# Three waiting score tiles move out of the shared wide slots, and the planner's DMA factor goes from 1.1 to 0.9

## The chip, the cores and the metric

One core of one Trainium2 chip runs the whole program. The metric is the device time of one execution in microseconds (us), taken as the median of several executions without a profiler. One further execution, recorded by the hardware profiler, gives the trace that is read here.

## The reference

Eight sequences of 3072 tokens go through an attention unit without a softmax and then through a maxout layer. Cut to what matters:

```python
# u, v: [8, 3072, 256]   z: [8, 3072, 64]   w1, w2: [256, 1024]   w_out: [1024, 256]
scores = (1 / 3072) * z @ z.T                 # per sequence, symmetric
attn   = maximum(scores, 0) ** 2
x      = u * (attn @ v)                       # [8 * 3072, 256]
out    = maximum(x @ w1, x @ w2) @ w_out      # [24576, 256]
```

## The kernel before

**Steps.** A sequence is cut into six groups of 512 tokens (four blocks of 128). One step computes one group's rows of the output, so there are 48 steps, n = 0 to 47, and sequence b = n // 6, group s = n % 6. The score matrix is symmetric: a block of scores that step i computes for a later group j (i < j) is transposed by a DMA (a "turn", job `("turn", n, k0)`, an SP instruction) and read again in step j. Only a few blocks of sequence 0 are computed directly instead (`direct`).

**A step's work.** TensorE (PE) makes score pairs `s_ps` (two blocks of 128 x 512, one PSUM pair), ScalarE (ACT) or VectorE (DVE) applies the relu into an A tile (`a_sb`, line 276 or 278) and one of them squares it in place (lines 282, 284). SP turns the squares into a T tile (`aT`), two turns for a tile of four blocks. Steps 0 to 2 are "plain": PE multiplies v by the A tiles directly. From step 3 on, the products follow a Strassen-like scheme with seven products for eight: DVE makes sums `es` of the A and T tiles (jobs S2, S3, S4, lines 290 and 293; S3 writes back into the tile), and PE runs products `Xa`, `Xb`, `Ya`, `Yb` over the step's six groups into `acc`. `add_ends` makes xT = u * acc; `add_second` or `add_seven` does the maxout layer for the step LAG = 3 behind: relu tiles `g_sb`, in most steps sums of them in `gs`, and the output tile `o_sb`, which SP stores to `out`. For b = 0 the turned tiles are those of (0,3), (0,4), (0,5), (1,3), (1,4), (1,5), (2,3), (2,4), (2,5), (3,4), (3,5), (4,5), where (i,j) is computed in step i and read in step j. Tiles of step 3 and later are turned after their S3, those of the plain steps right after the square.

**Buffers.** A tiles and T tiles of 4 KB per partition share WIDE = 19 slots (`share_wide`): by the planner's modelled times each tile gets the slot that comes free first, and it waits for all users of the tile that had the slot before. The output pool `opool` has two buffers of the same size, used in rotation (first by a staging tile `zf`, then by the output tiles of steps 0, 1, 2, ...). The pool `gspool` has one buffer for `gs`.

**Held tiles.** With HELD = 1, the tiles (0,4) and (0,5) of step 0 are called held: they take wide slots of their own (`a_held`), and the T tiles for them are ordered as if taken one microsecond into step 2 (`at_step(0, key[1] + 2, 1)`). Their turns may so be issued late, while the A tile keeps its slot.

**Planner.** PE's order is written out by hand (`pe_order`). All other engines' orders come from a list scheduler in the kernel's Python (`find_orders`): each job has a cost, a lag and a due time worked back from PE's plan, and at each point the job that can start first, or among nearly equal ones the one due first, is put next on its engine. The engines then run their queues in that order, each instruction waiting for its own semaphores. All DMAs, from SP and from POOL (GpSimd, which issues the loads of u, v, z and the weights), share one modelled queue:

```python
dma_free[0] = max(dma_free[0], begin + DMA_START[...]) + DMA_PART * j.dma
j.done = dma_free[0] + DMA_END
idle_from["SP"] = max(begin + SP_ISSUE, dma_free[0] - DMA_AHEAD)   # SP's DMAs only
```

with `DMA["turn"] = 1180` ns, `DMA_START` 870 (SP) or 1770 (POOL), `DMA_END` 1330, `DMA_AHEAD` 4500, `SP_ISSUE` 1450. The plan is made in 24 rounds, and the one that ends first by the model is kept.

Of the kernel before, what the change touches and what calls it, by code (L numbers as in the profile page):

```python
# [11 lines left out]
def kernel(  # L12
# [19 lines left out]
    bf16 = mybir.dt.bfloat16  # L32
# [7 lines left out]
    P = 128  # L40
    NSB = S // P
    G = 4
    WIN = 3
    GW = G * P
# [25 lines left out]
    widepool = ctx.enter_context(tc.tile_pool(name="widepool", bufs=1))  # L70
# [3 lines left out]
    gspool = ctx.enter_context(tc.tile_pool(name="gspool", bufs=1))  # L74
    opool = ctx.enter_context(tc.tile_pool(name="opool", bufs=2))
# [85 lines left out]
    def direct(b, i, j):  # L161
        return b == 0 and i < j <= NDIR
# [16 lines left out]
    q.zT = zpool.tile([P, NSB + 1, P], bf16, name="zT")  # L179


    HELD = 1
    ALONE, XB_TO, YA_FROM, YA_FIRST, O_CLEAR = 4, 2, 2, 6, 2


# [12 lines left out]
    TURN, TURN_LAG, UT_LAG = 1750, 4000, 7000  # L198

    DMA = dict(turn=1180, uT=1130, zT=4220, w2T=3800, store=1940, v=1680, u=1680, z=3130, w1=4100, w2=3000, wo=3500)  # L200
    DMA_SMALL, DMA_PART = 970, 1.1
    DMA_START, DMA_END, DMA_AHEAD, SP_ISSUE = {"SP": 870, "POOL": 1770}, 1330, 4500, 1450
    FIRST_LOADS = {("v", 0, 0): 0, ("v", 0, 1): 1200, ("v", 0, 2): 2500, ("v", 0, 3): 3700, ("v", 0, 4): 4900, ("v", 0, 5): 7700, ("u", 0): 6300}

# [17 lines left out]
    jobs, bufs, order = {}, {}, {}  # L222

    def job(key, ways, fn, deps=(), new=None, uses=(), after=(), lag=100):
        assert key not in jobs, key
        jobs[key] = Job(key, ways, fn, deps, new, uses, after, lag)

    def buf(pool, key, make):
        bufs[pool, key] = Buf(make)
        order.setdefault(pool, []).append(key)  # L230

    def tile_of(pool, key):
        return bufs[pool, key].tile
# [27 lines left out]
    def score(q, out_ps, j, k, s, q0, n):  # L261
        half = ds(j * dqk, dqk)
        matmul(
            out_ps,
            q.zT[half, k + 1 - j, :],
            q.zT[half, ds(G * s + 1 - j + q0, n), :],
            start=True,
            stop=True,
        )

    def turn(out_ap, in_ap):
        sp_dma(out=out_ap, in_=in_ap, transpose=True)

    def relu(eng, out_ap, in_ap):
        if eng == "ACT":
            pin(nc.scalar.activation(out_ap, in_ap, AF.Relu))  # L276
        else:
            pin(nc.vector.tensor_single_scalar(out=out_ap, in_=in_ap, scalar=0.0, op=ALU.max))

    def square(eng, ap):  # L280
        if eng == "ACT":
            pin(nc.scalar.activation(ap, ap, AF.Square))  # L282
        else:
            pin(nc.vector.tensor_mul(ap, ap, ap))  # L284
# [16 lines left out]


    def a_key(n, g):
        return ("T", ("held", n, g)) if n < HELD and g > 3 else ("A", (n, g))

    def a_tile(st, g):
        return tile_of(*a_key(st.n, g))
# [3 lines left out]
    def a_half(tile, k0):  # L311
        return tile[:, ds(k0 % G, 2), :].rearrange("p k x -> p (k x)")

    def a_rows(st, k0):
        return a_half(a_tile(st, k0 // G), k0).rearrange("p (t m x) -> p m t x", t=2, m=2)
# [84 lines left out]
    def s_tile(key):  # L400
        return tile_of("mm", key)

    def by_tokens(s_ps):
        return s_ps.rearrange("p m (t x) -> p m t x", t=2)
# [4 lines left out]
    def add_pair(st, k0, head=None):  # L409
        n, q, g = st.n, st.q, k0 // G  # L410
        key = (n, k0)
        first = k0 % G == 0
        if first:
            if a_key(n, g)[0] == "A":
                buf("A", (n, g), lambda tag: widepool.tile([P, G, GW], bf16, name="a_sb", tag=tag))
            else:
                bufs[a_key(n, g)] = Buf(lambda tag: widepool.tile([P, G, GW], bf16, name="a_held", tag=tag))

        def scores(_):
            for j in range(2):  # L420
                score(q, s_tile(key)[:, j, :], j, k0 + j, st.s, 0, G)

        job(("score", n, k0), {"PE": 223}, scores, deps=z_deps(st), new=("mm", key), lag=150)

        def do_relu(eng):
            relu(eng, a_rows(st, k0), by_tokens(s_tile(key)))

        def do_square(eng):
            square(eng, a_half(a_tile(st, g), k0))

        a = a_key(n, g)
        job(
            ("relu", n, k0),
            RELU,
            do_relu,
            deps=[("score", n, k0)],
            new=a if first else None,
            uses=[("mm", key), a],
            after=() if first else [("relu", n, k0 - 2)],
            lag=200,  # L440
        )
        job(("square", n, k0), SQUARE, do_square, deps=[("relu", n, k0)], uses=[a], lag=200)
        if g > st.s and not direct(st.b, st.s, g):
            t = ("T", (st.b, st.s, g))
            if first:
                turned_order.append((("score", n, k0), t[1]))
                bufs[t] = Buf(lambda tag: widepool.tile([P, G, GW], bf16, name="aT", tag=tag))

            def do_turn(_):
                turned = a_half(tile_of(*t), k0)  # L450
                turn(turned.rearrange("p (s x) -> p s x", x=P), a_half(a_tile(st, g), k0))

            job(
                ("turn", n, k0),
                {"SP": TURN},
                do_turn,
                deps=[("square", n, k0) if first or st.plain else ("S3", n, g)],
                new=t if first else None,
                uses=[a, t],
                after=() if first else [("turn", n, k0 - 2)],  # L460
                lag=TURN_LAG + (5000 if st.plain else 0),
            )
# [467 lines left out]
    def add_seven(st):  # L930
# [111 lines left out]
        for name, ways, fn, deps, after, new, uses in (  # L1042
            ("osn", {"ACT": 470}, lambda e: held(), [("o", n, 1)], [], ok, [pair, ok]),
            ("oe1", {"DVE": 336}, lambda e: sub(C(0, 1), slot(1), C(0, 0)), [("osn", n)], [], None, [pair, ok]),
            ("onf", {"DVE": 336}, lambda e: sub(C(1, 1), C(1, 1), slot(3)), [("o", n, 3)], [], None, [pair, ok]),
            ("ok", {"DVE": 336}, lambda e: add(C(0, 0), C(1, 1), slot(0)), [("onf", n)], [], None, [pair, ok]),
            ("oe3", {"DVE": 336}, lambda e: sub(C(1, 1), slot(1), C(1, 1)), [("onf", n)], [("ok", n)], None, [pair, ok]),
            ("oe0", {"DVE": 336}, lambda e: add(C(0, 0), C(0, 0), slot(2)), [("ok", n)], [("oe3", n)], None, [pair, ok]),
            ("oe2", {"ACT": 270}, lambda e: copy("ACT", C(1, 0), slot(2)), [("o", n, 3)], [], None, [pair, ok]),
        ):  # L1050
            job((name, n), ways, fn, deps=deps, new=new, uses=uses, after=after, lag=200)
# [241 lines left out]
    turned_order = []  # L1293
# [135 lines left out]
    for i, w in enumerate(work):  # L1429
        key = w[2]  # L1430
# [43 lines left out]
    def pe_job_at(ns):  # L1474
        found = [key for key, at in zip(pe_order, pe_at) if at >= ns]
        return [found[0]] if found else [pe_order[-1]]


    def at_step(b, s, us):
        return pe_job_at(starts[NG * b + s] + us * 1000)  # L1480
# [13 lines left out]
    def z_deps(st):  # L1494
        return [("zT", st.b)] if st.b else []
# [130 lines left out]
    for st in steps:  # L1626
        for k0 in st.rows:
            add_diag(st) if k0 is None else add_pair(st, k0)
# [22 lines left out]
    for k0 in (0, 2, 4, 6):  # L1651
        bufs["mm", (0, k0)] = Buf(psum_pair)
    order["mm"] = [(0, k0) for k0 in (0, 2, 4, 6)] + order["mm"]
    for pool in ("acc0", "acc1"):
        order[pool].sort(key=lambda k: k[0] * 2 + k[1] if isinstance(k, tuple) else 2 * k)
    position = {key: i for i, key in enumerate(pe_order)}
    order["A"].sort(
        key=lambda k: position.get(("score", k[0], None if k[1] == steps[k[0]].s and steps[k[0]].diag else G * k[1]), -1)
    )
    def held(key):  # L1660
        return a_key(key[1], key[2] // G)[0] == "T"

    slots = sorted(
        [
            (position[at_step(0, key[1] + 2, 1)[0]] if held(key) else position.get(key, -1), k)
            for key, k in turned_order
        ]
        + [(position.get(key, -1), ("held", key[1], k[2])) for key, k in turned_order if held(key)]
        + [(position[at_step(0, 0, 7)[0]], "w2"), (position[at_step(0, 1, 7)[0]], "w2T")],
        key=lambda x: x[0],  # L1670
    )
# [3 lines left out]
        A=NA, T=NT, es=6, v=6, lf=5, xT=LAG, g=2, o=2, e0=1, gs=1, xs=1, u=2, uT=2, mm=1000, acc0=1, acc1=1  # L1675
# [306 lines left out]
```

## Time and profile before

| | |
|---|---|
| median of 3 executions | 910.29 us (909.14 to 910.53) |
| profiled execution, own time | 914.21 us |
| its span in the trace | 912.4 us |
| mean granted TensorE clock | 0.996 |
| PE / DVE / ACT / POOL busy | 892.1 / 790.0 / 756.2 / 58.4 us |
| DMA moved | 146.65 MB, mean 161 GB/s |

The profiled execution is 3.92 us longer than the median of the executions without a profiler. PE is busy for 98% of the span. A "window" of the profile is a stretch of the span with the busy time of every engine in it; the granted clock there is the share of full TensorE speed. A DMA issue on SP is shown with the time it kept SP's queue, which includes its wait for semaphores; "to landing" is the time from its issue until the data has arrived.

### The profile page before, as it was taken

Reading aid. Unit: us, or ns where it says so; the run is one execution under the profiler, and the core shown is the slowest. Engines: PE = TensorE matmul, PEld = TensorE weight load, DVE = VectorE, ACT = ScalarE, POOL = GpSimd, SP = SyncE. Lnnn points to the kernel's source line nnn. Section 1 sums busy time; section 2 is a strip of 40 time slices with the busy share of each in tenths; the row PEclk is TensorE's granted clock in tenths of the full one; section 3 lists DMA queues with packets and bytes.
Section 4 is the critical chain, followed back from the end, with each engine's and each line's share of the span. In section 5 each row is a group of like instructions: output and inputs, shape, how many; then the busy total and the mean of one; then the engine's idle time right before and its main releaser. Section 6 shows DMA issues by size and latency. Waiting matters only on the chain.

```text
span 912.4 us, 37105 instructions
## 1 busy us (share of the span) xinstructions
PE 892.1 (98%) x16333; PEld 745.5 (82%) x16333; DVE 790.0 (87%) x1703; ACT 756.2 (83%) x944; POOL 58.4 (6%) x115
## 2 busy tenths in 40 slices
PE   9999799999999999999999999999999999999998
PEld 3368688887888888888788888888888898888885
DVE  6777678988989999999899899998999899989970
ACT  7967699778997899888997889977999779997634
POOL 2101000010000000001000010000000001000000
PEclk9999899999999999999999999999999999999999
DMA  9999999999999999999999999999989999999711
GB/s 156 130 167 175 186 182 173 175 163 159 153 169 190 164 183 149 164 185 167 165 146 164 183 169 151 166 169 173 183 138 178 179 178 152 170 160 162 123 61 70
DMA packets 382930, 146.65 MB, mean 161 GB/s; under 512 B 361264, under 2 KB 362928, under 8 KB 382768
## 3 DMA queue, kind: packets, MB, share of 16 engines
q1 hardware_dynamic: 366208, 114.54, 79.3%
q0 software_dynamic: 16560, 29.74, 23.5%
q8 instruction: 127, 2.08, 1.0%
q14 instruction: 35, 0.29, 0.1%
HBM read 59.77 MB, written 25.17 MB: 93 GB/s over the span
## 4 chain that ended last, share of the span: by engine, by line
PE 74%; DVE 12%; DMA 6%; ACT 4%; issue 2%; SPq 0%; POOL 0%; DVEq 0%; POOLq 0%; ACTq 0%
PE s_ps L87 37%; PE acc L87 37%; DMA v_sb<-in_v_dram 3%; DMA aT<-a_sb 3%; DVE es L290 2%; ACT a_sb L276 2%; DVE es L293 2%; DVE a_sb L293 1%; ACT g_sb L276 1%; DVE xT L297 1%; DVE e L290 1%; DVE e L293 1%; DVE a_sb L284 1%; DVE o_sb L293 1%; DVE gs L293 1%
## 5 line engine op out<-in xcount | busy, mean ns | idle before, releaser
L87 PEld LDWEIGHTS <-v_sb 64*128 64x128 bf16 (+1 forms) x4464 | 336.1, 94 | 68.9 <-issue 15.2
L276 ACT ACTIVATE a_sb<-s_ps 128x1024 bf16<-128x1024 f32 x337 | 303.8, 943 | 45.4 <-PE s_ps L87 43.8
L87 PEld LDWEIGHTS <-lf 64*128 64x128 bf16 x3240 | 266.2, 94 | 21.9 <-issue 7.3
L87 PE MATMUL acc<-es,v_sb 64*128 64x256 bf16 x2160 | 279.0, 269 | 0.0
L87 PE MATMUL acc<-es,lf 64*128 64x256 bf16 x1080 | 246.6, 269 | 0.3
L87 PE MATMUL acc<-a_sb,lf 64*128 64x256 bf16 x1224 | 233.1, 269 | 1.0 <-issue 1.0
L87 PE MATMUL s_ps<-xT,w_sb 64*128 64x512 bf16 (+1 forms) x1484 | 214.0, 377 | 0.0
L282 ACT ACTIVATE a_sb<-a_sb 128x1024 bf16<-128x1024 bf16 (+1 forms) x217 | 211.1, 993 | 2.3
L276 ACT ACTIVATE g_sb<-s_ps 128x1024 bf16<-128x1024 f32 x187 | 185.9, 1024 | 8.6 <-PE s_ps L87 6.9
L87 PE MATMUL acc<-aT,lf 64*128 64x256 bf16 x936 | 180.1, 271 | 3.8 <-DMA aT<-a_sb 3.1
L87 PE MATMUL acc<-a_sb,v_sb 64*128 64x256 bf16 (+1 forms) x1352 | 145.4, 280 | 3.2 <-DVE e L290 2.3
L87 PE MATMUL s_ps<-zT 64*128 64x512 bf16 (+2 forms) x774 | 122.5, 337 | 6.1 <-DVE o_sb L290 2.9
L290 DVE TENSOR_TENSOR es<-aT 128x1536 bf16<-128x1536 bf16 (+1 forms) x117 | 106.5, 933 | 1.3 <-DMA aT<-a_sb 1.2
L87 PEld LDWEIGHTS <-gs 64*128 64x128 bf16 x2688 | 99.1, 94 | 9.5 <-issue 1.3
L87 PEld LDWEIGHTS <-w_sb 64*128 64x128 bf16 (+1 forms) x1488 | 80.9, 94 | 26.0 <-POOLq L95 1.0
L87 PEld LDWEIGHTS <-g_sb 64*128 64x128 bf16 x2336 | 91.6, 94 | 10.4 <-POOLq L95 7.1
L284 DVE TENSOR_TENSOR a_sb<-a_sb 128x1024 bf16<-128x1024 bf16 (+1 forms) x121 | 74.8, 625 | 25.9 <-ACT a_sb L276 25.9
L87 PE MATMUL acc<-aT,v_sb 64*128 64x256 bf16 x936 | 89.5, 272 | 0.0
L293 DVE TENSOR_TENSOR es<-a_sb 128x512 bf16<-128x512 bf16 x198 | 79.1, 421 | 9.6 <-PE acc L87 9.5
L87 PE MATMUL s_ps<-wf_sb,gs 64*128 64x128 bf16 x2016 | 81.2, 216 | 0.5 <-issue 0.5
L87 PE MATMUL s_ps<-w_out_sb,g_sb 64*128 64x128 bf16 (+1 forms) x1664 | 78.8, 226 | 0.0
L290 DVE TENSOR_TENSOR es<-a_sb 128x1024 bf16<-128x1024 bf16 x108 | 72.4, 687 | 0.0
(84 smaller groups left out, 1079.6 us busy)
## 6 DMA issues: line engine op xcount, KB each, us to landing
out_dram<-o_sb SPq DMA_DIRECT2D x47, 512.0 KB, 5.5
v_sb<-in_v_dram POOLq DMA_DIRECT2D x48, 256.0 KB, 6.0
u_sb<-in_u_dram POOLq DMA_DIRECT2D x48, 256.0 KB, 5.7
aT<-a_sb SPq DMA_TRANSPOSE x230, 5.3
z_sb<-in_z_dram POOLq DMA_DIRECT2D x7, 384.0 KB, 7.0
w_sb<-in_moe_w_dram POOLq DMA_DIRECT2D x2, 512.0 KB, 10.3
uT<-u_sb SPq DMA_TRANSPOSE x48, 5.6
a_sb<-a_sb SPq DMA_TRANSPOSE x45, 5.5
```

The lines of the kernel that those rows point to most:

```text
L87: newest[0] = pin(nc.tensor.matmul(*args, **kw)).ins
L276: pin(nc.scalar.activation(out_ap, in_ap, AF.Relu))
L282: pin(nc.scalar.activation(ap, ap, AF.Square))
L284: pin(nc.vector.tensor_mul(ap, ap, ap))
L290: pin(nc.vector.tensor_add(*args))
L293: pin(nc.vector.tensor_sub(*args))
L297: nc.vector.scalar_tensor_tensor(out=out_ap, in0=in0, scalar=c2, in1=in1, op0=ALU.mult, op1=ALU.mult)
```

## The change

The tiles (0,4) and (0,5) are now built in `opool`, under the name and in the buffers of the output tiles, and the tile (1,5) of step 1 is built in `gspool`, in the buffer of `gs`. None of the three takes a wide slot any more; (1,5) had an ordinary A slot before. The output tiles of steps 0 and 1 come after (0,4) and (0,5) in the rotation of the output pool, and the first `gs` comes after (1,5). The T tiles for (0,4) and (0,5) are ordered one microsecond into step 1, and the T tile for (1,5) nine microseconds into step 1 (TURNED_AT); before, the one for (1,5) was ordered at the tile's own scores. The planner's factor DMA_PART, by which each transfer's own part of the modelled DMA queue is multiplied, goes from 1.1 to 0.9, for all 48 steps.

```diff
-    HELD = 1
+    HOMES, TURNED_AT = {(0, 4): "o", (0, 5): "o", (1, 5): "gs"}, {0: (1, 1), 1: (1, 9)}
...
-    DMA_SMALL, DMA_PART = 970, 1.1
+    DMA_SMALL, DMA_PART = 970, 0.9
...
     def a_key(n, g):
-        return ("T", ("held", n, g)) if n < HELD and g > 3 else ("A", (n, g))
+        return (HOMES[n, g], ("held", n, g)) if (n, g) in HOMES else ("A", (n, g))
...
-        if first:
-            if a_key(n, g)[0] == "A":
-                buf("A", (n, g), lambda tag: widepool.tile([P, G, GW], bf16, name="a_sb", tag=tag))
-            else:
-                bufs[a_key(n, g)] = Buf(lambda tag: widepool.tile([P, G, GW], bf16, name="a_held", tag=tag))
+        a = a_key(n, g)
+        if first and a[0] == "A":
+            buf("A", (n, g), lambda tag: widepool.tile([P, G, GW], bf16, name="a_sb", tag=tag))
+        elif first:
+            home, name = {"o": (opool, "o_sb"), "gs": (gspool, "gs")}[a[0]]
+            buf(*a, lambda: home.tile([P, G, GW], bf16, name=name))
...
+    for pool in ("o", "gs"):
+        order[pool].sort(key=lambda k: (not isinstance(k, tuple), k))
...
     slots = sorted(
         [
-            (position[at_step(0, key[1] + 2, 1)[0]] if held(key) else position.get(key, -1), k)
+            (position[at_step(0, *TURNED_AT[key[1]])[0]] if a_key(key[1], key[2] // G)[0] != "A" else position.get(key, -1), k)
             for key, k in turned_order
         ]
-        + [(position.get(key, -1), ("held", key[1], k[2])) for key, k in turned_order if held(key)]
```

More of the change, by code (lines that the diff above doesn't have):

```diff
@@ L429, in do_square @@
             square(eng, a_half(a_tile(st, g), k0))
-        a = a_key(n, g)
         job(
@@ L1659 @@
     )
-    def held(key):
-        return a_key(key[1], key[2] // G)[0] == "T"
     slots = sorted(
         [
-            (position[at_step(0, key[1] + 2, 1)[0]] if held(key) else position.get(key, -1), k)
+            (position[at_step(0, *TURNED_AT[key[1]])[0]] if a_key(key[1], key[2] // G)[0] != "A" else position.get(key, -1), k)
             for key, k in turned_order
         ]
-        + [(position.get(key, -1), ("held", key[1], k[2])) for key, k in turned_order if held(key)]
         + [(position[at_step(0, 0, 7)[0]], "w2"), (position[at_step(0, 1, 7)[0]], "w2T")],
```

## The prediction

> **What bounds the kernel now.** I read the page first, then PE's windows, the waits around the one place where PE is not full, and the DMA view on both sides of it.
>
> ```profile
> span 912.4 us, 37105 instructions
> PE 892.1 (98%) x16333; PEld 745.5 (82%) x16333; DVE 790.0 (87%) x1703; ACT 756.2 (83%) x944; POOL 58.4 (6%) x115
> ```
>
> PE is the bound: it is idle for 912.4 - 892.1 = 20.3 us in all. A change that adds no matmul can only win that idle time, and time in which PE runs below full clock. The windows of two microseconds show where both lie together (columns: stretch, then length and busy time with count for PE, PEld, DVE, ACT, POOL, then granted clock, DMA share, GB/s):
>
> ```profile
> core 0: us, PE busy (x) PEld busy (x) DVE busy (x) ACT busy (x) POOL busy (x), PEclk, DMA share, GB/s
> 100.00:102.00 2.00, 1.12 (x20) 0.82 (x15) 2.00 (x5) 0.00 (x0) 0.00 (x0) 1.00 0.95 327
> 102.00:104.00 2.00, 0.70 (x12) 0.60 (x12) 1.97 (x5) 1.34 (x3) 0.00 (x0) 1.00 1.24 279
> 104.00:106.00 2.00, 0.24 (x5) 0.04 (x1) 1.17 (x3) 1.58 (x2) 0.00 (x0) 1.00 1.25 95
> 106.00:108.00 2.00, 1.12 (x10) 0.77 (x11) 1.36 (x3) 0.26 (x1) 0.00 (x0) 0.50 1.20 253
> 108.00:110.00 2.00, 2.00 (x16) 1.14 (x14) 1.87 (x4) 1.82 (x2) 0.00 (x0) 0.50 0.94 213
> 110.00:112.00 2.00, 2.00 (x22) 1.64 (x20) 0.64 (x1) 1.02 (x1) 0.68 (x2) 0.50 1.05 259
> 112.00:114.00 2.00, 2.00 (x24) 1.43 (x22) 0.05 (x1) 0.76 (x3) 0.37 (x1) 0.79 1.27 114
> ```
>
> The idle time of the first four windows is 0.88 + 1.30 + 1.76 + 0.88 = 4.8 us. Then the clock falls: PE's busy time at 0.50 and 0.79 loses 1.12 x 0.5 + 2 x 0.5 + 2 x 0.5 + 2 x 0.21 = 3.0 us. This one place, the start of step 5, costs 7.8 us. The waits there say what came last, and the timelines of ACT, SP, DVE and PE where it came from (start, length, what, and in brackets the idle time before it):
>
> ```profile
> ACT o_sb L287 <- DMA out_dram<-o_sb: 4.4, 1, 4.4
> PE acc L87 <- DMA aT<-a_sb: 2.6, 1, 2.6
> PE s_ps L87 <- ACT o_sb L287: 2.2, 1, 2.2
> ```
>
> ```profile
> 59.16 0.43 DVE L293 TENSOR_TENSOR es<-aT 128x512 bf16<-128x512 bf16 x1 [2.27 <-DMA aT<-a_sb]
> 59.80 3.88 SPq L104 DMA_TRANSPOSE aT<-a_held  x2
> 63.72 0.59 ACT L287 COPY o_sb<-s_ps 128x512 f32<-128x512 f32 x1 [5.01 <-PE s_ps L87]
> 72.36 3.66 SPq L104 DMA_TRANSPOSE aT<-a_held  x1
> 79.78 0.59 ACT L287 COPY o_sb<-s_ps 128x512 f32<-128x512 f32 x1 [3.47 <-PE s_ps L87]
> 81.09 1.30 SPq L104 DMA_TRANSPOSE aT<-a_held  x1
> 84.28 0.42 DVE L293 TENSOR_TENSOR a_sb<-es,a_sb 128x512 bf16<-128x512 bf16 x1
> 95.80 0.58 SPq L104 DMA_DIRECT2D out_dram<-o_sb  x1
> 96.47 9.26 SPq L104 DMA_TRANSPOSE aT<-a_sb  x4
> 102.66 1.07 ACT L287 COPY o_sb<-s_ps 128x512 f32<-128x512 f32 x2 [4.39 <-DMA out_dram<-o_sb]
> 106.88 0.40 PE L87 MATMUL acc<-aT,lf 64*128 64x256 bf16 x2 [2.65 <-DMA aT<-a_sb]
> ```
>
> Both late things are SP's. The store of step 0's output was ready after the copies of 63.72 and was issued at 95.80; step 2's copy needs its buffer, waited 4.39 us, and PE's next score waited 2.2 us behind it. Then PE waited 2.65 us for a turned tile. The four turns of 96.47 are by my count of the turned tiles the last ones, (3,5) and (4,5); the S3 of (4,5) is the DVE row of 84.28, so these turns were ready some 12 us before SP came to them. What stood ahead of them in SP's queue includes the four turns of the held tiles: 3.88 + 3.66 + 1.30 = 8.8 us of it.
>
> **Part 1: the three tiles.** The edit adds and removes no instruction: the same relus, squares, products and six turns. What moves is time and place. The held tiles' T slots are asked for 1 us into step 1 instead of step 2, so their four turns can be issued before step 3 instead of at 59.80 to 81.09. Is there room on SP ahead of that? SP's own waits and the DMA view between 20 and 57 us, then the DMA view between 57 and 107:
>
> ```profile
> SPq L104 <- DVE a_sb L284: 12.2, 3, 6.1
> SPq L104 <- PE s_ps L87: 7.7, 1, 7.7
> SPq L104 <- DVE es L290: 4.5, 1, 4.5
> ```
>
> ```profile
> q0 software_dynamic: 2160, 2.75, 59.6%
> q1 hardware_dynamic: 10146, 2.52, 58.1%
> aT<-a_sb SPq DMA_TRANSPOSE x7, 7.9
> ```
>
> ```profile
> q1 hardware_dynamic: 26254, 7.01, 92.2%
> aT<-a_held SPq DMA_TRANSPOSE x4, 4.6
> ```
>
> SP waits for semaphores for 12.2 + 7.7 + 4.5 = 24.4 of those 37 us, and its DMA queue (q1) moves 2.52 / 37 = 0.07 MB/us, against 7.01 / 50 = 0.14 MB/us from 57 to 107. A turn moves 128 x 1024 x 2 B = 0.262 MB, so at the later rate it takes 1.87 us, and four take 7.5 us: near the 8.8 us that they kept SP. Taking them out of the second stretch brings the store of 95.80 and the turns behind it forward by 7.5 to 8.8 us, which is more than both late arrivals (4.39 and 2.65 us). So I count the whole stall as gone, idle and clock: -7.8 us. What is late next there is not nothing; the nearest row is the same place one step earlier:
>
> ```profile
> 80.00:85.00 5.00, 4.52 (x82) 4.05 (x79) 4.44 (x10) 3.17 (x5) 0.02 (x1) 1.00 1.06 221
> ```
>
> PE idles 0.48 us there with the clock at 1.00: I add 0.5 us. The bounds are 0 (nothing late) and 7.8 us (the stall stays).
>
> The clock's 3.0 us rest on the windows alone. The Trainium skill (TensorE: Matmul & The Clock Gate, Part 1: The HAM clock gate) says that about 3.4 us of idling halve the clock and about 3.4 us of sustained work restore it. This trace agrees on the half (0.50 granted) but not on the return: PE was full from 108 on and was at 0.50 until 112. By the page the clock term would be 3.4 x 0.5 = 1.7 us and the forecast 1.3 us higher.
>
> **What it adds.** In the first stretch the four turns run beside loads: a turn there landed after 7.9 us, in the median of seven, where the held ones took 4.6 later. Step 3's first sums already wait for a turn there (2.27 us before 59.16). If one of the four delays those, a turn's length at the fastest rate of the trace is the nearest price; the GB/s row of 58 to 66 us, in 40 slices, gives it:
>
> ```profile
> GB/s 291 288 266 257 223 209 130 0 79 223 204 209 211 201 169 237 207 198 92 4 0 0 3 8 10 10 47 287 284 273 270 220 218 183 172 181 227 198 210 209
> ```
>
> 0.262 MB at 291 to 209 GB/s is 0.90 to 1.25 us: I add 1.0 us. The bounds are 0 (SP's 24.4 us of waits take it) and 4 x 1.87 = 7.5 us (all four stand ahead of step 3's turns).
>
> The new homes bring new waits. ACT's output copies of 63.72 and 79.78 now also wait until (0,4) and (0,5) have been turned. That costs nothing if the turns are issued before step 3; ACT's queue, with the relus behind the copy, pays if they are not (the third rival). The `gs` buffer is first needed by a sum in step 6, the tile is read last in a turn of step 1 or 2: nothing. The freed wide slots can only bring A and T tiles forward: I count no gain beyond the stall.
>
> **Part 2: the factor.** Each turn is reckoned at 1180 x 0.9 = 1062 ns of the queue instead of 1298. The first lies within the 0.90 to 1.25 us of the slices above, the second just over it; both lie under the 1.87 us of a busy mixed stretch. So the plan becomes right for an unshared queue and more optimistic for a shared one. From step 6 on it reshuffles DVE, ACT and SP. The rows of that part:
>
> ```profile
> 160.00:870.00 710.00, 700.48 (x13801) 609.61 (x13797) 655.71 (x1423) 610.44 (x768) 42.82 (x81) 1.00 1.08 166
> aT<-a_sb SPq DMA_TRANSPOSE x190, 5.3
> DVE lf L290 <- DMA v_sb<-in_v_dram: 4.3, 3, 2.4
> PE s_ps L87 <- DVE o_sb L290: 2.9, 5, 0.6
> ```
>
> PE is idle for 710 - 700.48 = 9.5 us: that is the most that better orders could win. The largest wait of PE after 110 us is 2.9 us in five pieces, for DVE; the only DMA for which DVE waits noticeably after 120 us is a load of v, 4.3 us. No turn is late there, so some margin stands, and I take 0, between -9.5 and the second rival's price.
>
> **Sum.** 914.21 - 7.8 + 0.5 + 1.0 = 907.9 us for the profiled execution. The median without a profiler is 3.92 us lower in the pair before, so 904.0 us.
>
> **Rivals.** *The cover of the factor is gone (slower).* A step after 160 us has 190 / 38 = 5 turns (38 steps of 18.7 us). If a step's five stand in one backlog, the last is planned 5 x 0.236 = 1.18 us earlier than now, the `es` sum that reads it is put earlier in DVE's queue, and all behind it waits. DVE idles (710 - 655.71) / 38 = 1.43 us per step, so it can take most of that, not all, since those gaps are not in the right place. If a quarter reaches PE, 42 steps from step 6 on lose 42 x 0.295 = 12.4 us; with the stall gone that is 904.0 + 12.4 = 916.4 us. It decides from 6.3 / 42 = 0.15 us per step on. For it: a turn lands 5.3 us after its issue in the median, while the model says 870 + 1062 + 1330 ns = 3.3 us when nothing is ahead (3.5 before). Against it: the same shortfall exists today, with no turn late after 110 us.
>
> *The stall only moves ahead.* The four turns queue up among the loads, weights and w2's transpose of 20 to 57 us, step 3 pays the 7.5 us bound instead of 1.0, and the sum is 914.21 - 7.8 + 0.5 + 7.5 = 914.4, or 910.5 us in the median: no change. For it: q0's 59.6% and the 7.9 us to landing; against it: SP's 24.4 us of waits. The Trainium skill (DMA: Bandwidth & Descriptors, Issuing engines are not separate DMA queues) says that transfers of all issuing engines end up on the same 16 DMA engines; the 7.9 against 4.6 us agrees, and it speaks for this rival.
>
> *The change does not do what it says.* The scheduler may keep the four turns where they are. Then the copy of 79.78 waits for the turn of 81.09, which lands 4.6 us later at 85.7: 5.9 us on ACT. The wait of 4.39 us cost PE 2.2, so this one costs some 2.9 us, with the old stall still there: 913.2 us. Against it: the wait enters the due times as well, which pulls those turns forward.
>
> **How the numbers follow.** Forecast 0.55, factor 0.23, stall moved 0.12, turns not moved 0.10. A measurement of this kernel can tell 0.2% (1.8 us) from no change. The forecast's own spread, from both added terms at 0 to both somewhat larger, stays below 908.5, so it is all faster; of the moved stall I give 0.04 to faster and 0.06 to same; of the factor rival 0.04 to same, since small shares of it land near the break-even point. That makes faster 0.59, same 0.10, slower 0.31. Low end: both added terms at 0 (902.5) and a third of the 9.5 us won by the new orders: 899.3 us. High end: the factor rival's 916.4 us. Outside lie a larger share of the factor rival and more luck with the orders, together 2 in 10. The likeliest case alone spans 900 to 908 us.
>
> **What would show it.** Right: PE full and the clock at 1.00 between 95 and 115 us; turns from the output buffers before 57 us; no wait of an output copy for a store; the (4,5) turns issued some 8 us earlier against step 5's start. The factor rival would show as DVE waiting for `aT` after 120 us, with more than 9.5 us of PE idle time between 160 and 870. The moved stall would show as PE idle or slow between 50 and 65 us. The third rival would show as ACT waiting for a turn before a copy into `o_sb`. The prediction is wrong if the stall is gone and the time is not lower, or if it stays.

## The result, and the profile after

The changed kernel takes 0.9914 of the time of the kernel before (95% interval 0.9889 to 0.9938, 20 executions of each): 7.8 us less of 910. The medians of all these executions are 903.89 us for the changed kernel and 914.0 for the kernel before; a second comparison on another chip gave 0.9908 (0.9875 to 0.994). Ratios leave out disturbed executions, and the rest of one kernel still spread over more than 10 us (896.43 to 909.74 us for the changed one), which matters below.

The profiled execution took 907.36 us, with a span of 905.6. The page's lines and the windows of PE where it is not full (same columns as before):

```profile
span 905.6 us, 37106 instructions
PE 887.9 (98%) x16333; PEld 743.3 (82%) x16333; DVE 788.7 (87%) x1701; ACT 754.9 (83%) x946; POOL 58.6 (6%) x115
```

```profile
102.00:104.00 2.00, 2.00 (x42) 2.00 (x38) 1.93 (x6) 1.62 (x3) 0.00 (x0) 1.00 1.03 283
104.00:106.00 2.00, 2.00 (x37) 1.79 (x35) 2.00 (x5) 1.49 (x3) 0.00 (x0) 1.00 1.50 113
106.00:108.00 2.00, 2.00 (x34) 1.67 (x32) 2.00 (x4) 2.00 (x3) 0.00 (x0) 1.00 2.28 257
```

The stall at the start of step 5 is gone: PE is full and its clock is whole. But there is a new one, at the start of step 3:

```profile
56.00:58.00 2.00, 1.89 (x26) 1.36 (x24) 0.00 (x0) 0.71 (x2) 0.00 (x0) 1.00 1.31 98
58.00:60.00 2.00, 0.00 (x0) 0.00 (x0) 0.00 (x0) 0.00 (x0) 0.00 (x0) 1.00 1.40 66
60.00:62.00 2.00, 0.61 (x4) 0.28 (x4) 0.00 (x0) 0.00 (x0) 0.00 (x0) 0.52 1.22 147
62.00:64.00 2.00, 0.58 (x3) 0.13 (x3) 1.75 (x5) 0.00 (x0) 0.00 (x0) 0.50 0.94 190
64.00:66.00 2.00, 1.91 (x20) 1.59 (x21) 1.97 (x5) 0.00 (x0) 0.00 (x0) 0.50 1.58 186
66.00:68.00 2.00, 2.00 (x32) 1.86 (x30) 1.93 (x7) 0.00 (x0) 0.00 (x0) 0.77 0.71 143
```

That is 5.0 us idle and, at the clocks shown, 2.0 us of slow work: 7.0 us, about what step 5 had lost. SP's queue and the waits tell why:

```profile
18.83 10.45 SPq L104 DMA_TRANSPOSE aT<-o_sb  x4
30.73 7.69 SPq L104 DMA_TRANSPOSE aT<-a_sb  x3
42.43 18.73 SPq L104 DMA_TRANSPOSE aT<-a_sb  x4
61.34 0.61 PE L87 MATMUL acc<-aT,v_sb 64*128 64x256 bf16 x4 [3.45 <-DMA aT<-a_sb]
62.25 0.42 DVE L293 TENSOR_TENSOR es<-aT 128x512 bf16<-128x512 bf16 x1 [8.86 <-DMA aT<-a_sb]
```

All four turns of the held tiles now go out at 18.83, as forecast, and the tiles that step 3 needs come later: the turns of (2,3) are in the group of 42.43, behind the two of (1,4) that nobody needs before step 4 (one of these is in that group, the other in the group of 30.73). PE and DVE wait for them. So within the first 107 us this execution won next to nothing: it was busy 44.99 of the 50 us from 57 to 107, against 44.60 before. That window ends before the slow clock of before does: from 107 on, PE at half clock until 112.8 costs the kernel before 2.9 us more. Counted by work instead of time, the 1500th matmul starts at 138.4 us before and at 135.4 us after, so 3.0 of the 6.8 us by which the spans differ are won up to the end of step 5, and 3.8 us come later. From 160 to 820 us:

```profile
160.00:820.00 660.00, 650.48 (x12786) 565.33 (x12781) 609.58 (x1324) 577.53 (x726) 41.23 (x78) 1.00 1.09 167
```

is the row of before, and

```profile
160.00:820.00 660.00, 653.27 (x12888) 568.48 (x12884) 613.03 (x1332) 577.39 (x727) 41.41 (x79) 1.00 1.08 168
```

that of after: 9.5 us of PE idle time became 6.7, where I had reckoned with no change.

### The profile page after: what moved, and what is told of

Read it like the earlier page. It is cut to its first block, busy times and chain, and to the rows that moved or that the text cites. A ratio compares the mean times of both kernels' runs of the same rounds, so it can differ in the third digit from the quotient of the medians.

```text
span 905.6 us, 37106 instructions
## 1 busy us (share of the span) xinstructions
PE 887.9 (98%) x16333; PEld 743.3 (82%) x16333; DVE 788.7 (87%) x1701; ACT 754.9 (83%) x946; POOL 58.6 (6%) x115
## 4 chain that ended last, share of the span: by engine, by line
PE 75%; DVE 12%; ACT 6%; DMA 3%; issue 3%; SPq 0%; POOL 0%; DVEq 0%; POOLq 0%
PE acc L87 38%; PE s_ps L87 37%; DVE es L290 2%; ACT g_sb L276 2%; DMA v_sb<-in_v_dram 2%; ACT a_sb L276 2%; DVE es L293 2%; DVE a_sb L293 1%; DVE e L290 1%; DVE xT L297 1%; DVE e L293 1%; DVE o_sb L293 1%; ACT a_sb L282 1%; DVE gs L293 1%; DMA z_sb<-in_z_dram 1%
## 5 line engine op out<-in xcount | busy, mean ns | idle before, releaser
L276 ACT ACTIVATE a_sb<-s_ps 128x1024 bf16<-128x1024 f32 (+1 forms) x335 | 301.6, 944 | 36.3 <-PE s_ps L87 34.6
L87 PE MATMUL acc<-a_sb,v_sb 64*128 64x256 bf16 (+1 forms) x1344 | 142.4, 279 | 1.9 <-DMA a_sb<-a_sb 1.2
L87 PE MATMUL s_ps<-zT 64*128 64x512 bf16 (+2 forms) x774 | 120.2, 333 | 2.5 <-DVE o_sb L290 1.2
L284 DVE TENSOR_TENSOR a_sb<-a_sb 128x1024 bf16<-128x1024 bf16 (+1 forms) x117 | 72.6, 625 | 23.7 <-ACT a_sb L276 23.5
L87 PE MATMUL acc<-aT,v_sb 64*128 64x256 bf16 x936 | 87.4, 270 | 3.5 <-DMA aT<-a_sb 3.5
```

The source lines that it names most:

```text
L87: newest[0] = pin(nc.tensor.matmul(*args, **kw)).ins
```

## The experiments

Theory A is that of the prediction: the homes empty SP's queue ahead of step 5, the factor is worth nothing. Rival B: the factor does it. The first four kernels take the change apart, by part and by stretch of the plan.

**The factor alone** (the kernel before with one line changed):

```diff
-    DMA_SMALL, DMA_PART = 970, 1.1
+    DMA_SMALL, DMA_PART = 970, 0.9
```

> Only the factor is changed (0.9); the three tiles stay where they were. Theory A (the prediction's): the homes empty SP's queue ahead of step 5, the factor is worth nothing by itself; then the stall of 7.8 us at the start of step 5 stays and the time is within 0.3% of the kernel before. Rival B (the factor does it): with every transfer reckoned shorter, the planner issues the store of step 0 and the last turns for step 5 earlier even with the held tiles in the wide slots; then the stall at step 5 is under 2 us, and the time is 0.6 to 1.0% lower.

Measured: 0.9963 (0.9933 to 0.9994). The stall at step 5 is gone (PE busy 24.92 of the 25 us from 95 to 120), which A did not allow, but step 3 has a worse one (15.72 of the 25 us from 50 to 75), with 8.6 us in one wait of PE:

```profile
PE acc L87 <- DVE xT L297: 8.8, 2, 8.6
```

Here the xT of step 2 waits for its uT, which SP issued behind five turns and w2's transpose. Neither theory is right as it stands: 0.9 repairs one place of the head (the first 110 us or so) and breaks another.

**The homes alone** (the changed kernel with the factor back at 1.1):

```diff
-    DMA_SMALL, DMA_PART = 970, 0.9
+    DMA_SMALL, DMA_PART = 970, 1.1
```

> Only the three tiles are moved; the factor stays 1.1. Theory A: the step 5 stall is gone (PE idle under 1.5 us from 95 to 115 us), the time is 0.6 to 1.0% lower. Rival B: the stall stays at 5 us or more including the slow clock, the time is within 0.3% of the kernel before.

Measured: 0.9952 (0.9916 to 0.9988). The head is full, at step 3 and at step 5:

```profile
50.00:75.00 25.00, 25.00 (x345) 18.84 (x345) 14.60 (x36) 16.71 (x23) 1.58 (x3) 1.00 1.12 174
95.00:120.00 25.00, 24.61 (x434) 20.89 (x432) 20.01 (x42) 22.50 (x27) 1.06 (x2) 1.00 1.15 196
```

This is A's mechanism, at somewhat more than half of the gain that A expected. At 1.1 only two of the held turns go out early, and those of (2,3) at 39.60, ahead of (1,4):

```profile
19.97 5.50 SPq L104 DMA_TRANSPOSE aT<-o_sb  x2
39.60 4.33 SPq L104 DMA_TRANSPOSE aT<-a_sb  x2
```

**The factor by stretch** (both from the changed kernel, in the line that lengthens the modelled queue):

```diff
-... + DMA_PART * j.dma
+... + (DMA_PART if begin < 110000 else 1.1) * j.dma      # early
+... + (DMA_PART if begin >= 110000 else 1.1) * j.dma     # late
```

> Both changes, but the factor 0.9 only for transfers that the plan begins in its first 110 us, 1.1 after that. If the gain lies in the first six steps, the time equals that of the whole change within 0.2%. If some 3 us come from the later steps' orders (the profile of the changed kernel gains 3.8 us after step 6), it is 0.3 to 0.4% slower than the whole change.

Measured: 1.0025 (0.9997 to 1.0053), 1.1% above the whole change and far more than expected.

> Both changes, but the factor 0.9 only for transfers that the plan begins after its first 110 us, 1.1 before that. If the gain lies in the homes, the time equals that of the whole change within 0.3%. If it needs 0.9 in the first six steps, the step 5 stall is back and the time is within 0.3% of the kernel before, less what the later orders give (some 3 us).

Measured: 0.9906 (0.9869 to 0.9942), as good as the whole change. So 0.9 is wanted after the first 110 us and not before. What it does there is little: between these plans and their partners with 1.1 in that stretch, the orders of PE, ACT, DVE and POOL are identical, and SP's 394 transfers differ in 32 swaps of neighbours. The plan's new times also change the shared wide slots a little: 13 to 15 of some 285 tiles follow another tile in their slot.

**The same late swaps on the kernel before**, beside the changed kernel and the late factor once more:

```diff
-... + DMA_PART * j.dma
+... + (0.9 if begin >= 110000 else 1.1) * j.dma
```

> The kernel before, tiles where they were, the factor 0.9 only after the first 110 us of the plan. The plan then differs from the kernel before in 32 swaps of neighbours in SP's order alone; the orders of PE, DVE, ACT and POOL are the same. If these swaps are what the later steps gained, PE idles under 5 us between 160 and 820 us (9.5 before), the step 5 stall stays, and the time is 0.4 to 1.0% lower. If the later gain is chance, the time is within 0.2% of the kernel before.

Measured: 0.9921 (0.9893 to 0.9949), with the three tiles where they had been. PE idles 5.6 us from 160 to 820, a little over what was expected. The step 5 stall was expected to stay, but it is small in this execution, although the first 110 us of the plan are those of the kernel before.

> The changed kernel itself, so that the kernels beside it are compared with it on the same chip: 0.9% below the kernel before, with a stall of some 7 us at step 3 (50 to 75 us) in the profile.

Measured: 0.9908 (0.9875 to 0.994); in this profile step 3 loses 3.3 us of idle time instead of 5.0 and keeps its clock.

> Homes moved, factor 1.1 in the first 110 us of the plan and 0.9 after. If the step 3 stall that 0.9 brings early is there in every execution and not in the profiled one alone, this is 0.5 to 0.8% faster than the changed kernel beside it. If the stall is an accident of the profiled execution, both times agree within 0.3%.

Measured: 0.99 (0.9867 to 0.9934), against 0.9908 beside it: not to be told apart. The step 3 stall is not there, but what it costs in the mean of executions is less than I thought.

**Urgent turns first.** In the changed kernel's SP order, the turns of (1,4) go behind those of (2,3):

```diff
+late = [x for x in emitted if x[0].key in (("turn", 1, 16), ("turn", 1, 18))]
+emitted = [x for x in emitted if x not in late]
+at = [x[0].key for x in emitted].index(("turn", 2, 14)) + 1
+emitted[at:at] = late
```

> The changed kernel, with one edit of SP's order: the two turns of tile (1,4), which step 4 reads, go behind the two of (2,3), which step 3 reads. Theory C (the early factor puts turns that are not urgent ahead of urgent ones): PE is busy for over 22.5 of the 25 us from 50 to 75 us (20.0 in the changed kernel) and the time is 0.3 to 0.5% lower than that of the changed kernel. Rival D (the loads of w_out, u and z make the turns slow, whatever the order): the stall keeps at least 5 of its 7 us and the time is the same.

Measured: 0.9912 (0.9886 to 0.9937). PE is busy for all 25.00 us from 50 to 75, so it was the order and not the loads, as far as one profile of each tells (the changed kernel's second profile has 21.72); but it idles 2.3 us from 95 to 120, and the time is that of the changed kernel. The mechanism of C is seen, its gain is not.

**Which of the 32 swaps?** In the trace of before a pattern stands out. Once or twice in a sequence SP issues a store of 512 KB within a microsecond after a load of v; at the worst of these places the load lands late, the fold that reads it waits on DVE, and PE waits for the sums `e` behind it. This place in the kernel before (POOL, SP, DVE, PE rows):

```profile
445.12 0.53 POOL L108 DMA_DIRECT2D v_sb<-in_v_dram  x1 [3.73 <-PE acc L87]
445.69 0.33 SPq L104 DMA_DIRECT2D out_dram<-o_sb  x1
453.19 0.42 DVE L290 TENSOR_TENSOR lf<-v_sb 128x512 bf16<-128x512 bf16 x1 [2.40 <-DMA v_sb<-in_v_dram]
455.72 0.40 PE L87 MATMUL acc<-a_sb,v_sb 64*128 64x256 bf16 x4 [1.72 <-DVE e L290]
```

In the changed kernel the transpose uT goes first there, and the store comes 3.0 us after the load:

```profile
440.93 0.53 POOL L108 DMA_DIRECT2D v_sb<-in_v_dram  x1 [3.73 <-PE acc L87]
442.62 1.23 SPq L104 DMA_TRANSPOSE uT<-u_sb  x1
443.96 0.52 SPq L104 DMA_DIRECT2D out_dram<-o_sb  x1
```

The median landing of the 36 loads and 35 or 36 stores of that stretch, before and after:

```profile
out_dram<-o_sb SPq DMA_DIRECT2D x35, 512.0 KB, 5.9
v_sb<-in_v_dram POOLq DMA_DIRECT2D x36, 256.0 KB, 5.9
```

```profile
out_dram<-o_sb SPq DMA_DIRECT2D x36, 512.0 KB, 4.7
v_sb<-in_v_dram POOLq DMA_DIRECT2D x36, 256.0 KB, 5.3
```

So the swaps were split on the kernel before, 19 with uT and a turn, 12 with a store (the 32nd, near the end, is in neither set). Both sets leave every tile in the slot that it had before:

```diff
+if kind == "store":                       # from step 6 on, neighbours only
+    if n % 6 == 2: yield ("store", n - 3), ("turn", n, 22)
+    if n % 6 == 0 and n > 6: yield ("store", n - 4), ("uT", n)
+else:
+    if n % 6 in (1, 3) and n < 45: yield ("turn", n, 22), ("uT", n + 1)
+    if n % 6 == 5: yield ("turn", n + 1, 4), ("uT", n)
```

> The kernel before, with only those of the late factor's swaps on SP's queue (from step 6 on) that put the transpose of u (uT) ahead of a turn; the stores stay where they were. Theory S (the stores matter: before, a store of 512 KB is issued within a microsecond of a load of v, and the fold that reads v waits on DVE): the median landing of the v loads from 160 to 820 us stays near 5.9 us, PE idles 8 us or more there, and the time is within 0.3% of the kernel before. Rival U (an earlier uT matters): the time is 0.5 to 0.9% lower, as with all swaps.

Measured: 0.9979 (0.9944 to 1.0014): no gain that can be told. Two of the expected numbers missed: the v loads land after 5.3 us all the same, and PE idles 6.9 us.

> The kernel before, with only those of the late factor's swaps on SP's queue that put a store behind the uT or the turn that followed it: 12 of 32 swaps. Theory S: the v loads land after 5.0 to 5.4 us in the median from 160 to 820 us, PE idles under 5 us there, and the time is 0.5 to 0.9% lower, as with all swaps. Rival U: within 0.3% of the kernel before.

Measured: 0.9913 (0.9879 to 0.9947): 12 swaps of neighbours give as much as the whole change, without its slots. The v loads land after 5.3 us, PE idles 5.0 us:

```profile
160.00:820.00 660.00, 655.02 (x12910) 569.05 (x12906) 614.73 (x1337) 580.19 (x731) 41.94 (x79) 1.00 1.09 168
```

Since the median landing does not separate these two, I counted in each trace, from 160 to 820 us, the stores that SP issues within 2 us after a load of v:

| kernel | stores met by a v load | PE idle 160 to 820, us | ratio |
|---|---|---|---|
| before | 11 | 9.5 | 1 |
| uT swaps only | 11 | 6.9 | 0.9979 |
| homes alone (1.1) | 10 | 14.7 | 0.9952 |
| homes, 0.9 early only | 9 | 8.5 | 1.0025 |
| six store swaps (below) | 4 | 4.7 | 0.9993 |
| homes, 0.7 late (below) | 3 | 4.1 | 0.9899 |
| whole change | 2 and 1 | 6.7 and 4.6 | 0.9914 and 0.9908 |
| urgent turns first | 1 | 4.0 | 0.9912 |
| factor alone (0.9) | 2 | 2.7 | 0.9963 |
| before, 0.9 late | 1 | 5.6 | 0.9921 |
| 12 store swaps | 1 | 5.0 | 0.9913 |
| homes, 0.9 late | 2 and 0 | 3.0 and 2.2 | 0.9906 and 0.99 |

The counts fall into two groups. PE's idle time goes with them roughly (6.9 us and more in the first four rows, 6.7 and less in the others), and PE's waits for DVE in that stretch go with them clearly: 4.2 to 6.0 us in the first four rows, 0.6 to 2.5 in the others. The times do not follow in every row. And the meeting alone costs a load little: in the kernel before, the 11 loads that met a store landed after 6.2 us in the median, the other 25 after 5.1, and the latest of all (10.4 us) had met none.

**The factor at 0.7 late** (0.9 replaced by 0.7 in the late kernel):

> Homes moved, factor 1.1 in the first 110 us of the plan and 0.7 after it: against 0.9 there, seven more swaps on SP's queue, six of them a uT ahead of a short turn, none of a store. Theory S: the same time as with 0.9 late (1.0% below the kernel before), within 0.3%. Rival U: another 0.1 to 0.2% lower. A theory of size (the nearer the factor to a turn's real part of the queue, the better): slower than with 0.9 late.

Measured: 0.9899 (0.9845 to 0.9954), with 3 such stores: the same as with 0.9. Between 0.9 and 0.7 the size of the factor makes no difference that can be told; with the 12 swaps above, this speaks for the stores' place in SP's order.

**Six of the twelve.** Only the stores that stood before a uT:

```diff
-    if n % 6 == 2: yield ("store", n - 3), ("turn", n, 22)
```

> The kernel before, with only six swaps on SP's queue: in steps 12, 18, 24, 30, 36 and 42 the store goes behind the uT that followed it; it was issued 0.6 us after a load of v there. If the meeting of store and v load is the whole of the later gain, the time is 0.6 to 0.9% lower, as with the 12 store swaps. If the six stores that go behind a turn carry the gain, it is within 0.2% of the kernel before; if both carry half, 0.3 to 0.5% lower.

Measured: 0.9993 (0.9953 to 1.0032). The interval excludes the gain of all twelve, and not a half of it. Four meetings are left, and the profile's PE idle time is 4.7 us, as low as with all twelve, while the times do not follow. The place shown above (the store of 445.69) is one of these six, and PE's waits for DVE are all but gone in this profile (160 to 820 us; the two rows of before, then the only one left):

```profile
PE s_ps L87 <- DVE o_sb L290: 2.9, 5, 0.6
PE acc L87 <- DVE e L290: 2.3, 3, 1.7
PE s_ps L87 <- DVE o_sb L290: 0.6, 1, 0.6
```

So this experiment ends the waits that the traces put down to the meeting, and the median time stays. One caution: the profiled execution, at 903.67 us, was the second fastest of the twelve (median 908.87), and this kernel ran on another chip than the one with all twelve swaps. That the stores' places carry the later gain is shown; that they do so by meeting loads of v is not, and how the gain is shared between the two sets of six stays open.

**The head, over all profiles.** Five of these kernels have the first 110 us of the kernel before, and four those of the homes at 1.1. PE's idle time from 50 to 75 and from 95 to 120 us, added:

| head of the plan | PE idle in both windows, us | mean |
|---|---|---|
| before; 0.9 late; uT swaps; 12 store swaps; six store swaps | 4.9, 2.5, 6.1, 3.8, 3.5 | 4.2 |
| homes at 1.1 early (alone, late twice, 0.7 late) | 0.4, 0.0, 1.2, 0.3 | 0.5 |
| homes at 0.9 early (whole change twice, early only) | 5.1, 3.5, 5.9 | 4.8 |
| 0.9 early without homes | 9.4 | |

These are single profiles. The mean granted clock, which every execution has, supports the first two rows: wherever a profile shows the half clock between the first and the last microseconds, it is at step 3 or step 5, and the clock was 0.998 or more in 10 of the 12 executions of the homes alone, against 15 of 32 of the kernel before beside them. For the third row it is mixed: 3 of 12 with the homes and 0.9 early only, but 13 of 20 and 8 of 11 for the changed kernel, whose early plan is the same.

## Why the prediction was right, and where its steps were not

The time came out where it was forecast: 0.9931 of before was predicted (904.0 of 910.29), 0.9914 measured. The steps behind it did not come out as they stood: in the first profile the head gave 3.0 us where 6.3 were forecast and the later steps 3.8 where none were. The errors cancelled, and that the number came out so near is luck. The microseconds (904.0 forecast, 903.89 measured) are nearer still by another accident: the kernel before, 910.29 us in three executions, took 914.0 in the median of twenty.

**The stall at step 5 goes: right in kind, too large in size.** "I count the whole stall as gone, idle and clock: -7.8 us." The held turns did leave the full stretch of SP's queue, and every kernel with the homes keeps its clock there and idles 2.3 us or less from 95 to 120. The clean case is that with 1.1 early, 0.4 us, since there no stall ahead of step 5 could have given SP time to catch up; with 0.9 and no homes step 5 is full as well (24.92 of 25 us), but behind a stall at step 3. But 7.8 us was one execution's loss. The five profiles with that same head lose 4.2 us of idle time in the mean, anywhere from 2.5 to 6.1. With the homes and 1.1 it is 0.5, so the homes are worth some 3.7 us of idle time, and the time of the homes alone says 0.48%, or 4.4 us.

**What it adds: 1.0 us taken, 5.0 us idle and 2.0 us of slow clock found** in the first profile, near the upper bound of 7.5 us that I had given; in the second profile it was 3.3 us and no slow clock. The rival "the stall only moves ahead" had the place and the price. Its cause was another: not the four turns among the loads (with 1.1 early, when only two of the four go out early, the homes cost step 3 nothing), but the early factor, with which the planner issues turns that are ready though not urgent. With 0.9 early the head is as idle as before the change (4.8 against 4.2 us).

**The factor: "I take 0". This is the step that failed.** I wrote that it "reshuffles DVE, ACT and SP" from step 6 on; it moves nothing but 32 pairs on SP and a few slots. And it is worth 0.8% there (0.5 to 1.1%), 7.2 us, on the kernel before by itself. I had looked for turns that come late, found none, and took the 9.5 us of PE idle time as a bound only. A row that could have led there was quoted: the only DMA that DVE noticeably waited for was a load of v, 4.3 us. I did not ask what those loads had run into.

**The slow rival, "the cover of the factor is gone"**, did not come: in the whole change, the factor alone, the late factor and 0.7, neither DVE nor PE has any wait for a turn from 110 to 860 us. The queue model's optimism did no harm there; with only neighbours in SP's queue changing places, it had little room to.

**The third rival** did not come either: no copy into `o_sb` was kept from starting while its PSUM data was ready. The trace does name a turn as what ended 12.0 us of ACT's idle time before the copy of 69.24, but that is the step 3 stall: PE's last matmuls for that copy ended at 69.2, so until then there was nothing to copy.

One reading of part 1 was wrong and cost nothing: the tile in the `gs` buffer was not turned in step 1 or 2 but at 72.27, after step 3 had begun; the first sum into `gs` came at 117.45.

The parts do not add up to one sum, since each is worth something else beside the others. Between the ratios above, the late factor gives 0.8% on the kernel before, 0.5% with the homes and 1.1 early (0.9952 to 0.9906), and 1.1% with the homes and 0.9 early (1.0025 to 0.9914). The early factor costs 0.7% with the homes and 1.1 late (0.9952 to 1.0025), 0.4% without the homes (0.9921 to 0.9963), and 0.1% in the change itself (0.99 to 0.9908). The homes give 0.5% with 1.1 throughout and with 0.9 throughout (0.9963 to 0.9914), and 0.2% with 0.9 late only (0.9921 to 0.99). Each of these ratios is known to some 0.3%, so some of the differences are within the noise; why 0.9 early costs so little in the change itself stays open.

No version ran clearly faster than the change: the late factor with the homes (0.9906 and 0.99) and with 0.7 (0.9899) have the better profiles, with spans of 896.3, 895.6 and 896.1 us against 905.6 and 901.1, but their intervals overlap that of the change.

## What to carry to other kernels

When one profiled execution shows a stall of several microseconds that hangs on DMA arrivals, ask for the same stretch in a second profile before pricing it: here the same program order lost between 2.5 and 6.1 us there. In a kernel whose DMA queue is nearly full, look not only for transfers that come late but for pairs that start together: a large store that nobody waits for, issued beside a load that a whole chain waits for, is worth trying one place later. Here that gave 0.9% for twelve stores and nothing that could be told for six of them, so measure it, and do not go by the trace alone. And a factor in a planner is an indirect tool: compare the orders that it makes before saying what it is for.

## What the runs showed of the hardware that was not expected

A load of 256 KB that was issued 0.6 us ahead of a store of 512 KB landed 7.9 us after its issue (445.12; the fold started at 453.19). It was the slowest of the 11 that met a store in that trace, and their median was 6.2 us, against 5.1 for those that met none.

The half clock lasted the same time in both stalls, though the stalls differ. By the granted shares of the windows it ran from 106.0 to 112.8 us in step 5 of before (0.50 in three windows, then 0.79) and from 60.1 to 66.9 in step 3 of after (0.52, then 0.50 in two, then 0.77): 6.8 us each. PE was full from 108 in the first and had steady work from 64.1 in the second, so the return came 4.8 us after that in one case and 2.8 in the other. In the other profiles with a half clock near these places it lasted 6.8 us (uT swaps), 3.4 (the homes with 0.9 early only, and both kernels with store swaps) or 10.2 (factor alone): one, two or three times 3.4 us. The Trainium skill (TensorE: Matmul & The Clock Gate, Part 1: The HAM clock gate) gives some 3.4 us of sustained work for the return, counted in a window that runs free of the work. The first case fits that, since 4.8 us hold one whole window of 3.4; so the prediction's remark that this trace did not agree on the return does not hold. The second return, after 2.8 us of steady work, came somewhat sooner than the page's figure.
